# A one-token attention and SwiGLU layer on one core: the first 2 MiB of wq in eight DMAs of 16 partitions, and the last batch of K in one DMA

## The chip, the core and the metric

The kernel runs on one core of one Trainium2 chip. The core has five instruction streams: TensorE (PE, with its weight loads shown apart as PEld), VectorE (DVE), ScalarE (ACT), GpSimd (POOL) and SyncE (SP). SP does no arithmetic here; it issues DMAs. The transfers themselves are carried out by 16 DMA engines, which move data between the chip's memory (HBM) and the on-chip SBUF of 128 partitions. The metric is the device time of one execution in microseconds; lower is better. The kernel before takes 140.36 us (median of three runs, 140.25 to 140.44).

## The reference

Four sequences, one new token each (B = 4, D = 1024). Layer norm, attention over the last 2048 positions of a cache with 32 query heads and 4 key/value heads of 128 values, output projection and residual; then layer norm, a SwiGLU block of width 3584, and residual. Everything is bfloat16.

```python
def _A_ref(x, k_cache, v_cache, wq, wo):
    W = min(4096, max(256, Sk // 4))                      # 2048 of Sk = 8192
    q = (x @ wq).reshape(B, Sq, Hq, Dh).transpose(0, 2, 1, 3)
    k = jnp.repeat(k_cache[:, :, Sk - W:, :], rep, axis=1)
    v = jnp.repeat(v_cache[:, :, Sk - W:, :], rep, axis=1)
    scores = jnp.einsum("bhqd,bhkd->bhqk", q, k) * (Dh ** -0.5)
    o = jnp.einsum("bhqk,bhkd->bhqd", softmax(scores), v)
    return o.transpose(0, 2, 1, 3).reshape(B, Sq, Hq * Dh) @ wo

def _B_ref(x, w1, w3, w2):
    return (silu(x @ w1) * (x @ w3)) @ w2

h  = x + _A_ref(layernorm(x), k_cache, v_cache, wq, wo)
h2 = h + _B_ref(layernorm(h), w1, w3, w2)
```

With four rows of activations, nearly all the bytes are weights and cache: 8 MiB of wq, 8 of K, 8 of V, 8 of wo, 7 each of w1, w3 and w2, some 55.6 MB in all, each byte used once.

## The kernel before, in words

All large transfers are issued by SP, from one list called `plan` (line 131), in the order wq, K, V, wo, w1, w3, w2. Each entry fills one of five SBUF slots of 4 MiB (the pool `stream`, line 58; `SLOT` is 16384 bfloat16 per partition). `load_next` (line 143) takes the next entry; the first five are issued at once (line 152) and the others each time TensorE has been through the tile that an earlier slot held, so SP waits there for TensorE.

`load_rows` (line 92) loads weights, one DMA for each number in `pieces`. Its view of a weight, `(p i) n -> p (i n)`, gives each partition a contiguous run of rows. The first entry of wq is two DMAs of 2 MiB (`pieces` is `[2, 2]`): 128 partitions with 16 KiB each. The second is one of 4 MiB. `load_k` (line 103) loads two batches of K into a slot, one DMA of 2 MiB each; in partition `pp * 4 + g` lie 64 consecutive positions of head `g`, 16 KiB. For the last batch this is cut: the first 60 positions go as before (line 112), and the last `JT = 4` positions, 1 KiB per partition, go in a second DMA (line 114) whose access pattern names the head first, `g pp x` instead of `pp g x`. This one puts position block `pp` of head `g` into partition `g * 32 + pp`, so for these four columns the partitions are in another order, and line 259 reads them with another pattern.

ACT issues five small DMAs at the start: the input x (line 151) and four pieces of x in another layout (line 162).

Every DMA counts its completion on a semaphore. There are eight for all the DMAs of SP and ACT, given out in turn in the order of the program; a DMA whose semaphore was used by an earlier one is issued only after that earlier one has landed. In the kernel before, the order is x, the first DMA of wq, the four pieces of x, the second and third DMA of wq, and then K: the first DMA of K waits for x, the second for the first DMA of wq, and so on.

TensorE's work follows the same order: the query projection (line 224), K transposed in blocks of eight (line 278) and copied out by DVE and ACT in turn (lines 282 and 284), the scores one unit behind (`emit_scores`, line 252, 16 units of 512 positions), softmax, the product with V (line 330), wo (line 357), w1 and w3 (line 406), w2 (line 436). In `emit_scores`, a unit is four matmuls of 512 columns, one per head; the last unit is four of 384 and four of 128, because of the other partition order in its last four columns.

Of the kernel before, what the change touches and what calls it, by code (L numbers as in the profile page):

```python
# [10 lines left out]
P = 128  # L11
# [8 lines left out]
def kernel(  # L20
# [13 lines left out]
    nc = tc.nc  # L34

    B, _, D = A_x.shape
    Hkv, Sk, Dh = A_k_cache.shape[1], A_k_cache.shape[2], A_k_cache.shape[3]
    Hq = A_wq.shape[1] // Dh
    REP = Hq // Hkv
    W = min(4096, max(256, Sk // 4))  # L40
# [26 lines left out]
    QD = P // JG  # L67
# [6 lines left out]
    IF = F // P  # L74
    PK = P // Hkv
    JK = W // PK
    JT = 4
    assert CQ == REP * Dh and HF <= 512 and CG == QD * KC and CF == QD * IF and IO == QD == Hq


# [11 lines left out]
    def load_rows(src, n, r0, pieces):  # L92

        t = stream.tile([P, SLOT], BF16, tag="s")
        i = 0
        for m in pieces:
            nc.sync.dma_start(  # L97
                out=t[:, i * n : (i + m) * n], in_=src[:, (r0 + i) * n : (r0 + i + m) * n]
            )
            i += m  # L100
        return [t[:, k * n : (k + 1) * n] for k in range(i)]

    def load_k(b):
        t = stream.tile([P, SLOT], BF16, tag="s")
        out = []
        for k in range(BS):


            v = t[:, k * JK * Dh : (k + 1) * JK * Dh]
            n = (JK - JT) * Dh if b + k == B - 1 else JK * Dh  # L110
            k_v = A_k_cache[b + k, :, Sk - W : Sk, :].rearrange("g (pp j) d -> pp g (j d)", pp=PK)
            nc.sync.dma_start(out=v[:, :n], in_=k_v[:, :, :n])
            if n < JK * Dh:
                nc.sync.dma_start(out=v[:, n:], in_=k_v.rearrange("pp g x -> g pp x")[:, :, n:])
            out.append(v)
        return out

    def load_v(b):
# [11 lines left out]
    N_Q, N_F = Hq * Dh, F  # L130
    plan = (
        [("wq", load_rows, (wq_v, N_Q, c, [2, 2] if c == 0 else [4])) for c in range(0, KC, RQ)]
        + [("k", load_k, (b,)) for b in range(0, B, BS)]
        + [("v", load_v, (b,)) for b in range(0, B, BS)]
        + [("wo", load_rows, (wo_v, D, c, [RO])) for c in range(0, IO, RO)]
        + [("w1", load_rows, (w1_v, N_F, c, [RQ])) for c in range(0, KC, RQ)]
        + [("w3", load_rows, (w3_v, N_F, c, [RQ])) for c in range(0, KC, RQ)]
        + [("w2", load_rows, (w2_v, D, 0, [16])), ("w2", load_rows, (w2_v, D, 16, [5, 4, 2, 1]))]
    )
    loaded = {}  # L140
    cursor = [0]
# [19 lines left out]
    for j in range(JG):  # L161
        nc.scalar.dma_start(
            out=x_q[QD * j : QD * (j + 1) : RS, :], in_=x_flat[:, j * CG : (j + 1) * CG]
# [7 lines left out]
    for c in range(2):  # L171
# [8 lines left out]
        out=xn[:], in0=x_sb[:], scalar1=mv[:, 0:1], scalar2=rstd[:, 0:1],  # L180
# [4 lines left out]
    for kc in range(KC):  # L185
# [8 lines left out]
    qz = act.tile([P, B, Hkv * QD + REP], BF16)  # L194
# [6 lines left out]
        out=perm[:].rearrange("p (h dq) -> p h dq", dq=JG),  # L201
        in_=ident[:].rearrange("p (dq h) -> p h dq", dq=JG),
# [7 lines left out]
    for j in range(2, JG):  # L210
        nc.vector.tensor_tensor(
            out=same[:, 0, :], in0=same[:, 0, :], in1=ident[:, j * QD : (j + 1) * QD], op=ALU.add
# [6 lines left out]
    for kc in range(KC):  # L219
        wq_t = loaded["wq"][kc]  # L220
        for hf in range(CQ // 512):
            for g in range(JG):
# [3 lines left out]
                    lhsT=xnT[:, kc, :],  # L226
                    rhs=wq_t[:, c0 : c0 + 512],
                    start=(kc == 0),
                    stop=(kc == KC - 1),
# [7 lines left out]
    for r in range(REP):  # L237
        nc.tensor.transpose(out=qt_ps[:, r, :], in_=q_sb[:, r * Dh : (r + 1) * Dh], identity=ident[:])  # L238
    nc.vector.tensor_copy(
        out=qz[:, :, : Hkv * QD].rearrange("p b (g z) -> p b g z", g=Hkv)[:, :, :, :REP],  # L240
        in_=qt_ps[:].rearrange("p r (g x) -> p x g r", g=Hkv)[:, :B, :, :],
# [4 lines left out]
    scores_ps = psA.tile([P, W], FP32, tag="scores")  # L246
    NJ = 512 // PK
    TB = 8
    units = [(b, n) for b in range(B) for n in range(NSB)]
    kT_tiles = []  # L250

    def emit_scores(u):
        b, n = units[u]
        js = NJ - JT if u == len(units) - 1 else NJ
        for j0, j1 in ((0, js), (js, NJ)):
            if j0 == j1:
                continue
            kT_v = kT_tiles[u][:, j0:j1, :].rearrange(
                "d j (pp g) -> d g j pp" if j0 == 0 else "d j (g pp) -> d g j pp", g=Hkv
            )  # L260
            for g in range(Hkv):
                nc.tensor.matmul(  # L262
                    scores_ps[QD * g : QD * (g + 1), n * 512 + j0 * PK : n * 512 + j1 * PK],
                    lhsT=qz[:, b, g * QD : (g + 1) * QD],
                    rhs=kT_v[:, g, :, :],
                    start=(b == 0),
                    stop=(b == B - 1),
                    skip_group_check=True,
                )

    nt = 0
    for u, (b, n) in enumerate(units):
        k_v = loaded["k"][b].rearrange("p (j d) -> p j d", d=Dh)
        kT = ktpool.tile([P, NJ, P], BF16, tag="kT")
        for t in range(NJ // TB):
            kt_ps = psA.tile([P, TB, P], BF16, tag=f"kt{nt % 4}")
            for jj in range(TB):
                nc.tensor.transpose(  # L278
                    out=kt_ps[:, jj, :], in_=k_v[:, n * NJ + t * TB + jj, :], identity=ident[:]
                )  # L280
            if nt % 2 == 0:
                nc.vector.tensor_copy(out=kT[:, t * TB : (t + 1) * TB, :], in_=kt_ps[:])  # L282
            else:
                nc.scalar.copy(out=kT[:, t * TB : (t + 1) * TB, :], in_=kt_ps[:])  # L284
            nt += 1
        kT_tiles.append(kT)
        if u >= 1:
            emit_scores(u - 1)
        if n == NSB - 1 and b % BS == BS - 1:
            load_next()  # L290
    emit_scores(len(units) - 1)


# [9 lines left out]
        out=Pm[:].rearrange("q (c jq) -> q jq c", jq=NSB), in_=scores_ps[:].rearrange("q (jq c) -> q jq c", jq=NSB),  # L303
# [22 lines left out]
    for b in range(B):  # L326
        v_t = loaded["v"][b]
        for g in range(Hkv):
            for j in range(NK):
                nc.tensor.matmul(  # L330
                    OT_ps[:, b, g * REP : (g + 1) * REP],
                    lhsT=v_t[:, g, j, :],
                    rhs=PT_sb[:, j, g * QD + b * REP : g * QD + (b + 1) * REP],
                    start=(j == 0),
                    stop=(j == NK - 1),
# [19 lines left out]
    for i in range(IO):  # L355
        for j in range(JG):
            nc.tensor.matmul(  # L357
                y_ps[QD * j : QD * (j + 1), :],
                lhsT=o4[:, i, :, :].rearrange("p b s -> p (b s)"),
                rhs=loaded["wo"][i][:, j * CG : (j + 1) * CG],  # L360
                start=(i == 0),
                stop=(i == IO - 1),
# [26 lines left out]
        out=hn[:], in0=h1[:], scalar1=tot[:, 0:1], scalar2=rstd2[:, 0:1],  # L389
# [5 lines left out]
        out=hnT[:].rearrange("p k x -> p (k x)"), in_=hn[:].rearrange("q (c k) -> q k c", k=KC)  # L395
# [5 lines left out]
    def gate_up(kind, out_ps):  # L401
# [27 lines left out]
        out=hgT[:].rearrange("p i x -> p (i x)"),  # L429
        in_=hg[:].rearrange("q s c -> q (s c)").rearrange("q (c i) -> q i c", i=IF),  # L430
# [3 lines left out]
    for i in range(IF):  # L434
        for j in range(JG):
            nc.tensor.matmul(  # L436
                y2_ps[QD * j : QD * (j + 1), :],
                lhsT=hgT[:, i, :],
                rhs=loaded["w2"][i][:, j * CG : (j + 1) * CG],
                start=False,  # L440
                stop=(i == IF - 1),
                skip_group_check=True,
# [35 lines left out]
```

## Time and profile before

| what | value |
|---|---|
| median of three runs | 140.36 us |
| the profiled execution's own time | 140.44 us |
| its span, first to last instruction | 138.4 us |
| around the span | 2.0 us |
| TensorE matmul busy | 69.9 us, 50% of the span |
| VectorE, ScalarE busy | 36.4 us, 29.2 us |
| bytes read from HBM | 55.59 MB, 402 GB/s over the span |
| share of the 16 DMA engines' span that SP's queue used | 95.3% |
| granted TensorE clock, mean | 0.775 |

The span runs from the first to the last instruction of the program; the profiled execution's own time is about 2 us more. Of the engines none is busy for much more than half of the span, while the queue of SP's DMAs occupies the DMA engines for nearly all of it. A DMA is cut into packets, each carried by one of the 16 engines; the trace records the start, length and size of every packet, and each engine's part of a DMA ends in a 4-byte packet that counts on the semaphore. "Landed" below means that this count arrived.

### The profile page before, as it was taken

What the parts mean: (1) busy time and instruction counts of PE and PEld (TensorE: products, weight loads), DVE (VectorE), ACT (ScalarE), POOL (GpSimd) and SP (SyncE); (2) the same over time, 40 slices, a digit from 0 to 9 for tenths busy, and PEclk for the clock granted to TensorE, in tenths of its full rate; (3) what the DMA queues carried; (4) which work ended last, traced back from release to release, by engine and by line L of the source; (5) the groups of instructions that cost most, each with busy time, mean ns of one, the idle gap of its engine ahead of it and who ended that gap; (6) DMA issues with size and microseconds to landing.
All of it is one profiled execution on the core that took longest, in us unless ns stands there. A gap on an engine that the chain in (4) does not pass through costs nothing.

```text
span 138.4 us, 2316 instructions
## 1 busy us (share of the span) xinstructions
PE 69.9 (50%) x1049; PEld 44.7 (32%) x1049; DVE 36.4 (26%) x63; ACT 29.2 (21%) x28; POOL 1.6 (1%) x7
## 2 busy tenths in 40 slices
PE   0152204799898989500595687136080440801940
PEld 0111001296565646200585565112030210301820
DVE  6430000133343434440400203500003980070001
ACT  0400000125473736449450000000006000000000
POOL 4000000000000000000000000000000000000000
PEclk9999999999999999955555559955559555595685
DMA  5999989999999999999999999999999999899940
GB/s 154 441 414 511 426 388 398 445 426 421 432 402 339 419 419 421 417 462 497 398 426 403 436 439 421 456 423 414 439 456 411 414 439 477 379 432 408 418 186 2
DMA packets 4905, 55.74 MB, mean 403 GB/s; under 512 B 380, under 2 KB 540, under 8 KB 2848
## 3 DMA queue, kind: packets, MB, share of 16 engines
q1 hardware_dynamic: 4856, 55.58, 95.3%
q8 instruction: 8, 0.13, 0.3%
q10 hardware_dynamic: 40, 0.02, 0.1%
q14 instruction: 1, 0.01, 0.0%
HBM read 55.59 MB, written 0.01 MB: 402 GB/s over the span
## 4 chain that ended last, share of the span: by engine, by line
DMA 68%; PE 23%; ACT 4%; SPq 1%; DVE 1%; issue 1%; ACTq 0%
DMA t<-in_B_w_dram 53%; DMA t<-in_A_wq_dram 15%; PE kt_ps L278 11%; PE scores_ps L262 5%; ACT kT L284 4%; PE q_ps L224 3%; PE g_ps L406 2%; SPq L97 1%; PE qt_ps L238 1%; PE y_ps L436 1%; DVE q_sb L234 1%; DVE res L446 0%; ACTq L284 0%
## 5 line engine op out<-in xcount | busy, mean ns | idle before, releaser
L284 ACT COPY kT<-kt_ps 128x1024 bf16<-128x1024 bf16 x16 | 16.0, 1013 | 13.8 <-PE kt_ps L278 13.8
L278 PE MATMUL kt_ps<-ident,t 128*128 128x128 bf16 x256 | 18.3, 232 | 0.0
L278 PEld LDWEIGHTS <-t 128*128 128x128 bf16 x256 | 16.0, 105 | 6.1 <-issue 6.1
L282 DVE COPY kT<-kt_ps 128x1024 bf16<-128x1024 bf16 x16 | 11.1, 692 | 16.9 <-PE kt_ps L278 16.9
L406 PEld LDWEIGHTS <-hnT 128*32 128x32 bf16 x128 | 5.4, 139 | 27.6 <-issue 25.3
L224 PE MATMUL q_ps<-t,xnT 128*4 128x512 bf16 x64 | 7.3, 623 | 11.9 <-DMA t<-in_A_wq_dram 11.9
L262 PE MATMUL scores_ps<-kT,qz 128*32 128x512 bf16 (+2 forms) x68 | 10.5, 581 | 2.8 <-ACT kT L284 2.8
L406 PE MATMUL u_ps<-t,hnT 128*32 128x448 bf16 x64 | 6.2, 569 | 10.8 <-DMA t<-in_B_w_dram 10.8
L406 PE MATMUL g_ps<-t,hnT 128*32 128x448 bf16 x64 | 6.2, 563 | 10.5 <-DMA t<-in_B_w_dram 10.5
L436 PE MATMUL y_ps<-t,hgT 128*32 128x256 bf16 x112 | 5.7, 368 | 8.6 <-DMA t<-in_B_w_dram 8.6
L330 PE MATMUL OT_ps<-PT_sb,t 128*128 128x8 bf16 x256 | 7.4, 168 | 1.8 <-issue 1.6
L330 PEld LDWEIGHTS <-t 128*128 128x128 bf16 x256 | 7.3, 104 | 2.0 <-issue 1.8
L436 PEld LDWEIGHTS <-hgT 128*32 128x32 bf16 x112 | 4.3, 127 | 10.4 <-issue 6.3
L224 PEld LDWEIGHTS <-xnT 128*4 128x4 bf16 x64 | 2.0, 111 | 16.3 <-issue 16.0
L316 PE MATMUL pt_ps<-Dm,Pm 128*128 128x128 bf16 x16 | 1.9, 311 | 9.3 <-DVE Dm L309 9.3
L420 DVE RECIPROCAL eg<-eg 128x896 f32<-128x896 f32 x1 | 5.8, 5752 | 0.0
L357 PE MATMUL y_ps<-t,o 128*32 128x256 bf16 x128 | 5.1, 337 | 0.8 <-DVE o L346 0.8
L234 DVE TENSOR_SCALAR q_sb<-q_ps 128x512 bf16<-128x512 f32 x1 | 0.7, 691 | 17.9 <-PE q_ps L224 17.9
L235 ACT ACTIVATE q_sb<-q_ps 128x512 bf16<-128x512 f32 x1 | 0.6, 597 | 21.4 <-DVE q_sb L234 21.4
L419 DVE TENSOR_SCALAR eg<-eg 128x896 f32<-128x896 f32 x1 | 0.6, 627 | 16.8 <-ACT eg L418 16.8
L302 ACT ACTIVATE Pm<-scores_ps,nmax 128x2048 bf16<-128x2048 f32 x1 | 4.8, 4784 | 0.0
L316 PEld LDWEIGHTS <-Pm 128*128 128x128 bf16 x16 | 1.6, 145 | 9.7 <-ACT Pm L302 9.7
(67 smaller groups left out, 39.8 us busy)
## 6 DMA issues: line engine op xcount, KB each, us to landing
t<-in_B_w_dram SPq DMA_DIRECT2D x4, 3584.0 KB, 34.3
t<-in_A_v_cache_dram SPq DMA_DIRECT2D x4, 2048.0 KB, 30.2
t<-in_A_wo_dram SPq DMA_DIRECT2D x2, 4096.0 KB, 27.5
t<-in_A_k_cache_dram SPq DMA_DIRECT2D x3, 2048.0 KB, 25.7
t<-in_A_wq_dram SPq DMA_DIRECT2D x2, 2048.0 KB, 9.5
t<-in_A_wq_dram SPq DMA_DIRECT2D x1, 4096.0 KB, 20.9
t<-in_B_w_dram SPq DMA_DIRECT2D x1, 4096.0 KB, 42.2
t<-in_A_k_cache_dram SPq DMA_DIRECT2D x1, 1920.0 KB
```

The costliest lines, as they stand in the source:

```text
L224: nc.tensor.matmul(q_ps[QD * g : QD * g + B, hf * 512 : (hf + 1) * 512], lhsT=xnT[:, kc, :], rhs=wq_t[:, c0 : c0 + 512], start=(kc == 0), ...
L262: nc.tensor.matmul(scores_ps[QD * g : QD * (g + 1), n * 512 + j0 * PK : n * 512 + j1 * PK], lhsT=qz[:, b, g * QD : (g + 1) * QD], rhs=kT_v ...
L278: nc.tensor.transpose(out=kt_ps[:, jj, :], in_=k_v[:, n * NJ + t * TB + jj, :], identity=ident[:])
L282: nc.vector.tensor_copy(out=kT[:, t * TB : (t + 1) * TB, :], in_=kt_ps[:])
L284: nc.scalar.copy(out=kT[:, t * TB : (t + 1) * TB, :], in_=kt_ps[:])
L302: nc.scalar.activation(out=Pm[:].rearrange("q (c jq) -> q jq c", jq=NSB), in_=scores_ps[:].rearrange("q (jq c) -> q jq c", jq=NSB), func=A ...
L316: nc.tensor.matmul(pt_ps[:, jj, :], lhsT=Pm[:, (jb * JPB + jj) * P : (jb * JPB + jj + 1) * P], rhs=Dm[:], start=True, stop=True)
L330: nc.tensor.matmul(OT_ps[:, b, g * REP : (g + 1) * REP], lhsT=v_t[:, g, j, :], rhs=PT_sb[:, j, g * QD + b * REP : g * QD + (b + 1) * REP], ...
L357: nc.tensor.matmul(y_ps[QD * j : QD * (j + 1), :], lhsT=o4[:, i, :, :].rearrange("p b s -> p (b s)"), rhs=loaded["wo"][i][:, j * CG : (j + ...
L406: nc.tensor.matmul(out_ps[QD * j : QD * (j + 1), hf, :HF], lhsT=hnT[:, k, :], rhs=loaded[kind][k][:, c0 : c0 + HF], start=(k == 0), stop=( ...
L420: nc.vector.reciprocal(out=eg[:], in_=eg[:])
L436: nc.tensor.matmul(y2_ps[QD * j : QD * (j + 1), :], lhsT=hgT[:, i, :], rhs=loaded["w2"][i][:, j * CG : (j + 1) * CG], start=False, stop=(i ...
```

## The change

Two parts. The first DMA of the program's list, 2 MiB of wq for 128 partitions, becomes eight DMAs, each for 16 partitions that lie eight apart (partitions 0, 8, 16, ..., 120; then 1, 9, ...; to 7, 15, ..., 127), 16 KiB in each partition. All other calls of `load_rows` are as they were. And K's last batch is loaded by one DMA like the other three: the split of its last four columns is gone, from the load and from `emit_scores`, whose last unit is again four matmuls of 512 columns.

```diff
-    JT = 4
...
         for m in pieces:
-            nc.sync.dma_start(
-                out=t[:, i * n : (i + m) * n], in_=src[:, (r0 + i) * n : (r0 + i + m) * n]
-            )
+            step = 8 if cursor[0] == 0 and i == 0 else 1
+            for p0 in range(step):
+                nc.sync.dma_start(
+                    out=t[p0:P:step, i * n : (i + m) * n],
+                    in_=src[p0:P:step, (r0 + i) * n : (r0 + i + m) * n],
+                )
             i += m
...
-            n = (JK - JT) * Dh if b + k == B - 1 else JK * Dh
-            k_v = A_k_cache[b + k, :, Sk - W : Sk, :].rearrange("g (pp j) d -> pp g (j d)", pp=PK)
-            nc.sync.dma_start(out=v[:, :n], in_=k_v[:, :, :n])
-            if n < JK * Dh:
-                nc.sync.dma_start(out=v[:, n:], in_=k_v.rearrange("pp g x -> g pp x")[:, :, n:])
+            nc.sync.dma_start(
+                out=v,
+                in_=A_k_cache[b + k, :, Sk - W : Sk, :].rearrange("g (pp j) d -> pp g (j d)", pp=PK),
+            )
...
-        js = NJ - JT if u == len(units) - 1 else NJ
-        for j0, j1 in ((0, js), (js, NJ)):
-            if j0 == j1:
-                continue
-            kT_v = kT_tiles[u][:, j0:j1, :].rearrange(
-                "d j (pp g) -> d g j pp" if j0 == 0 else "d j (g pp) -> d g j pp", g=Hkv
-            )
-            for g in range(Hkv):
-                nc.tensor.matmul(
-                    scores_ps[QD * g : QD * (g + 1), n * 512 + j0 * PK : n * 512 + j1 * PK],
-                    lhsT=qz[:, b, g * QD : (g + 1) * QD],
-                    rhs=kT_v[:, g, :, :],
-                    start=(b == 0),
-                    stop=(b == B - 1),
-                    skip_group_check=True,
-                )
+        kT_v = kT_tiles[u][:].rearrange("d j (pp g) -> d g j pp", g=Hkv)
+        for g in range(Hkv):
+            z0 = (b * Hkv + g) * QD
+            nc.tensor.matmul(
+                scores_ps[QD * g : QD * (g + 1), n * 512 : (n + 1) * 512],
+                lhsT=qz[:, b, g * QD : (g + 1) * QD],
+                rhs=kT_v[:, g, :, :],
+                start=(b == 0),
+                stop=(b == B - 1),
+            )
```

SP issues 30 DMAs afterwards instead of 24: eight in place of one at the start, and one fewer in K. Since the eight semaphores are given out in turn, the waits at the start move too. Of the eight pieces the first three wait for nothing; the fourth waits for x, the fifth for piece 1, the sixth, seventh and eighth for the first, second and third small piece of x, and the second DMA of wq for the fourth small piece. The third DMA of wq then waits for piece 2, and the four DMAs of K for pieces 3 to 6. TensorE has eight fewer instructions (four weight loads and four matmuls).

## The prediction

> **What bounds the kernel now.** I read the slices first, then the chain of waits, then windows around the two edits, then SP's waits and the end of the timeline.
>
> ```profile
> PE   0152204799898989500595687136080440801940
> DMA  5999989999999999999999999999999999899940
> GB/s 154 441 414 511 426 388 398 445 426 421 432 402 339 419 419 421 417 462 497 398 426 403 436 439 421 456 423 414 439 456 411 414 439 477 379 432 408 418 186 2
> ```
>
> The DMA engines are busy from the first slice (3.46 us each) to the last but one; PE has holes everywhere. The chain of waits still hands a middle part to PE:
>
> ```profile
> 1.64 20.91 DMA t<-in_A_wq_dram
> ...
> 56.25 36.04 DMA t<-in_B_w_dram
> ...
> 96.40 37.66 DMA t<-in_B_w_dram
> ```
>
> Between 22.55 and 56.25 the chain runs through TensorE, because w1's first DMA is issued at 56.25, when TensorE gives a slot free. But it lands only 36 us later, behind transfers issued before it (wo's two DMAs land at 73 and 83). So TensorE could be many microseconds later without starving the queue. The end is the start of the byte stream, plus its length, plus a fixed tail. The tail starts where the last 256 KB of w2 land, at 134.69:
>
> ```profile
> 134.10 1.04 PE L436 MATMUL y_ps<-t,hgT 128*32 128x256 bf16 x12 [0.65 <-DMA t<-in_B_w_dram]
> ...
> 135.19 0.42 DVE L446 CAST res<-y_ps 128x256 bf16<-128x256 f32 x1 [11.55 <-PE y_ps L436]
> 135.64 0.61 SPq L447 DMA_DIRECT2D out_dram<-res  x1
> ```
>
> From 134.69 to the end of the span (138.40) it is 3.71 us, which the change does not touch.
>
> **The stream's own prices.** In the packet records a 16 KiB packet takes 611 ns (26.8 GB/s for one of the 16 engines), a 15 KiB one 573 ns, a 1 KiB one 46 ns where nothing disturbs it, a semaphore packet 9 ns. A 2 MiB DMA is eight 16 KiB packets per engine, 4.9 us. The windows show the one place where the stream sags after its start:
>
> ```profile
> 36.00:38.00 2.00, 2.00 (x32) 1.55 (x32) 0.69 (x1) 0.37 (x1) 0.00 (x0) 1.00 1.00 428
> ...
> 42.00:43.60 1.60, 1.00 (x10) 0.30 (x7) 0.14 (x1) 0.89 (x1) 0.00 (x0) 1.00 1.05 265
> 43.60:45.00 1.40, 1.40 (x27) 1.40 (x27) 0.69 (x1) 0.35 (x1) 0.00 (x0) 1.00 1.04 410
> ```
>
> The last columns are the share of DMA time and GB/s: 265 instead of 428 with every engine busy. It is the K remainder of line 114. Its 128 packets of 1 KiB lie on only four engines (four semaphore packets instead of sixteen), from 41.36 to 42.96; 0.6 us after its start V's 4 KiB packets on the other twelve go from 159 to between 270 and 300 ns, the 1 KiB packets from 46 to between 62 and 88, and all recover 0.6 us after its end. The four engines' counts arrive 0.8 to 0.9 us after their semaphore packets; elsewhere about 0.34. So data had been taken in and waited to be written: it is the SBUF side that was full.
>
> **Part one, K: gained.** For twelve engines V's first DMA took 5.61 to 5.66 us against 4.97 for its second: 0.64 too long. They also get back their share of K's last rows, 8 x (611 - 573) = 0.30 us. Net -0.33. The four engines of the remainder need 6.87 us from the end of K's main part to the end of V's first DMA, which becomes 4.97 + 0.30: -1.6. Following packets by their ends (the next begins 3 to 4 ns before), the landings of w2's last piece are: four engines by 132.53, eleven from 133.68 to 133.93, one at 134.69. Eight of the eleven are ordinary engines that each carried one of the eight 16 KB instruction fetches (some 1.4 us each); three are remainder engines. The one at 134.69 is the fourth, which also met an 8 KB fetch at 83.59. With -1.6 it drops to 133.1, and the eight set the end at 133.93 - 0.33 = 133.6: -1.1 us. If V's slow start had another cause, they end at 133.93 + 0.30 = 134.2: -0.46. I take -1.1, since the sag has the remainder's length and place. TensorE's last unit (four matmuls near 0.6 us instead of four of 384 and four of 128 columns) is hidden behind a queue of over 25 us; without that cover it would be some tenths of a microsecond.
>
> **Part two, the eight pieces.** Bytes and packets are the same; seven more semaphore packets per engine are 7 x 9 ns = 0.06 us. Nothing starts earlier: the first DMA is issued at 0.73 and its first packet starts at 1.75, while x, with four packets, is issued at 0.74 and starts at 1.68. Two costs have no row of their own.
>
> The first is SP's waiting. Now:
>
> ```profile
> SPq L112 <- DMA t<-in_A_wq_dram: 5.0, 1, 5.0
> ...
> SPq L112 <- DMA x_sb<-in_A_x_dram: 0.2, 1, 0.2
> ```
>
> Here SP sat 5 us for a landing with 10 MiB issued, and the engines stayed busy. With pieces, piece 4 waits for x (landed 2.39), piece 5 for piece 1 (by 3.6), pieces 6 to 8 and wq's second DMA for x's four small pieces, which landed at 7.3, 8.1, 9.2 and 10.4 because on their four engines they stood behind 16 KiB packets. Behind the waiting SP stands all of wq, K and V. But with short queues the small pieces pass sooner: five pieces keep the engines until 1.75 + 1.2 (the first packet) + 4 x 0.61 = 5.4, by then nothing stands before the small ones, and they land by 5.75 (0.34 later); piece 6 then starts about 1 us after its issue, at 6.8. So the stall is 0 to 1.4 us; I take 0.1, as each engine's small packets should slip in between two pieces, and none if the pieces are slow.
>
> The second is the rate. A piece names 16 partitions, eight apart, so the 16 engines write to a part of SBUF at a time. The normal row is 611 ns per packet: 0. The row of the only large DMA here that confines engines to few partitions is the K remainder: 32 KiB per engine from 41.37 to 43.90, less the usual 0.34, is 2.2 us, or 14.9 GB/s instead of 26.8. At that rate eight packets take 8 x 1.10 = 8.8 us instead of 4.9: +3.9. The window's 265 GB/s would make 7.9 us, +3.0; without taking off the 0.34, 10.1 us, +5.2. I take +3.9: strided pieces on a write-limited side are nearer to the remainder than to a DMA of all partitions, though 1 KiB packets are not 16 KiB ones.
>
> [...]
>
> Sum: +3.9 + 0.06 - 1.1 = +2.9 us. The profiled execution took 140.44, span 138.40 and 2.04 around, 0.08 above the median; on the median 140.36 this is 143.3.
>
> **Rivals.**
>
> *Full rate, 0.27.* If the sag came from 1 KiB packets or from HBM, 16 KiB pieces run at 611 ns each, and the K gain remains: -1.1 + 0.16 = -0.9, 139.4 (139.0 to 140.2 with the -0.46 and a short stall). For it: 16 KiB is the size that runs at 26.8 GB/s everywhere else. Against it: the counts of the remainder came late, which a slow read would not do. This is the faster side, and it decides wherever the pieces cost less than 1.0 us.
>
> *SP starves the engines, 0.10.* The pieces run at full rate but are issued too late: stall 1.4, or up to 3 if half the engines have nothing until piece 5 arrives (its issue 3.6 plus 1.0, against 1.75). With -1.1 to -0.46 that is 140.6 to 142.5, middle 141.5. For it: the waits for x's small pieces, 7.3 to 10.4 before. Against it: these were late because of the queue that is now absent.
>
> *The split does nothing visible* is part of the first rival: its gain is then K's alone.
>
> **How the numbers follow.** Slow pieces 0.63, time 143.3, its own range 142.3 (+3.0 - 1.1) to 145.0 (+5.2 - 0.46). Full rate 0.27, starved 0.10. About 0.2%, 0.28 us, is what a measurement here tells from no change: of the full-rate case 0.23 is faster and 0.04 within; of the starved case 0.01 is within. Faster 0.23, same 0.05, slower 0.72. The range has to take in the middle of the full-rate case: 139.3 to 145.0, leaving out less than 2 in 10.
>
> **What would show it.** Slow pieces: the first two slices of GB/s near 150 and 240, q_ps waiting for wq's first rows until about 11.5 to 12 instead of 8.14, the second landing about 4 later than 12.92, all later landings shifted alike. Full rate: first matmul of L224 near 8. Starved: DMA digits under 9 in the second slice. K: no window near 42 to 46 below 400 GB/s, and the end less late than the start by about 1 us. I am wrong if the pieces go at 428 GB/s, or if the sag near V's first DMA stays without the remainder.

## The result, and the profile after

The changed kernel takes 145.0 us (median of six runs, 144.16 to 145.88) against 140.33: 1.033 of the kernel before, 95% interval 1.028 to 1.039. The prediction said slower, by 2.9 us to 143.3; it is slower by 4.67 us, just past the top of the stated range, which is 4.64 us (145.0 on 140.36). The six times are not spread evenly: three lie at 144.2 to 144.3 and three at 145.7 to 145.9. Runs more than 1.5% above the fastest of the same kernel are left out of the ratios, here one of 148.91 us, of the pieces alone. The profiled execution belongs to the lower group: 144.16 us, span 142.2.

The 40 slices of the changed kernel, busy share of the DMA engines in tenths and GB/s (a slice is 3.55 us):

```profile
DMA  5998999999999999999999999999999999998950
GB/s 141 224 221 300 447 443 433 396 420 443 438 438 391 416 421 422 416 423 527 443 406 410 424 408 459 408 444 436 411 444 432 420 436 486 415 424 365 424 229 2
```

The engines are as busy as before, yet the second and third slice move 224 and 221 GB/s where the kernel before had 441 and 414. An engine counts as busy for as long as its packet takes, and here a 16 KiB packet takes 1.22 us instead of 0.61. In finer windows of the changed kernel (the last two columns are DMA share and GB/s; a window counts a packet's bytes and time where the packet begins, so a short one scatters):

```profile
3.50:5.50 2.00, 0.00 (x0) 0.00 (x0) 0.31 (x2) 1.38 (x2) 0.00 (x0) 1.00 1.07 223
5.50:7.50 2.00, 0.64 (x8) 0.56 (x8) 1.28 (x7) 0.19 (x1) 0.00 (x0) 1.00 0.88 199
7.50:9.50 2.00, 0.00 (x0) 0.00 (x0) 0.91 (x6) 0.00 (x0) 0.00 (x0) 1.00 1.05 229
9.50:12.00 2.50, 0.00 (x0) 0.00 (x0) 0.00 (x0) 0.00 (x0) 0.00 (x0) 1.00 0.96 216
12.00:14.00 2.00, 0.79 (x8) 0.27 (x12) 0.00 (x0) 0.00 (x0) 0.00 (x0) 1.00 0.88 360
```

Half the rate until the eight pieces are through, near 12 us. The packet records say it packet by packet: from 3.4 to 10.9 us a 16 KiB packet takes 1222 ns at the median, where it took 611 before. TensorE's first matmuls on wq (timeline of the changed kernel) show what is late:

```profile
13.21 1.88 PE L225 MATMUL q_ps<-t,xnT 128*4 128x512 bf16 x16 [6.07 <-DMA t<-in_A_wq_dram]
18.06 1.88 PE L225 MATMUL q_ps<-t,xnT 128*4 128x512 bf16 x16 [2.97 <-DMA t<-in_A_wq_dram]
27.75 3.58 PE L225 MATMUL q_ps<-t,xnT 128*4 128x512 bf16 x32 [7.81 <-DMA t<-in_A_wq_dram]
```

Before, these stood at 8.14, 12.92 and 22.59: 5.1 us later, each of them. The end of the timeline has the same form as before, with the last piece of w2 at 138.35 instead of 134.69, 3.7 us later:

```profile
137.78 1.02 PE L431 MATMUL y_ps<-t,hgT 128*32 128x256 bf16 x12 [0.78 <-DMA t<-in_B_w_dram]
138.84 0.42 DVE L441 CAST res<-y_ps 128x256 bf16<-128x256 f32 x1 [11.62 <-PE y_ps L431]
139.29 0.70 SPq L442 DMA_DIRECT2D out_dram<-res  x1
```

So of 5.1 us lost in the first 18 us, about 1.5 came back by the end. And SP's own waits in the changed kernel name a new kind:

```profile
SPq L99 <- DMA x_q<-in_A_x_dram: 2.3, 2, 1.7
SPq L99 <- DMA t<-in_A_wq_dram: 1.3, 1, 1.3
```

SP waits for the small pieces of x between the pieces of wq, as the order of the semaphores said it would.

### The profile page after: what moved, and what is told of

Same layout as the page of the kernel before. It is cut to its first block, busy times and chain, and to the rows that moved or that the text cites. A ratio compares the mean times of both kernels' runs of the same rounds, so it can differ in the third digit from the quotient of the medians.

```text
span 142.2 us, 2317 instructions
## 1 busy us (share of the span) xinstructions
PE 68.9 (48%) x1045; PEld 43.6 (31%) x1045; DVE 36.3 (26%) x63; ACT 29.0 (20%) x28; POOL 1.6 (1%) x7
## 4 chain that ended last, share of the span: by engine, by line
DMA 69%; PE 19%; ACT 5%; ACTq 2%; SPq 1%; issue 1%; DVE 1%
DMA t<-in_B_w_dram 52%; DMA t<-in_A_wq_dram 13%; PE kt_ps L273 8%; ACT kT L279 5%; PE scores_ps L258 5%; DMA x_q<-in_A_x_dram 4%; PE q_ps L225 3%; PE g_ps L401 2%; SPq L99 1%; ACTq L163 1%; PE y_ps L431 1%; DVE q_sb L235 0%; ACT q_sb L236 0%; ACTq L152 0%; DVE res L441 0%
## 5 line engine op out<-in xcount | busy, mean ns | idle before, releaser
L273 PE MATMUL kt_ps<-ident,t 128*128 128x128 bf16 x256 | 16.5, 219 | 0.0
L273 PEld LDWEIGHTS <-t 128*128 128x128 bf16 x256 | 14.4, 98 | 5.0 <-issue 4.9
L258 PE MATMUL scores_ps<-kT,qz 128*32 128x512 bf16 x64 | 9.9, 609 | 3.1 <-ACT kT L279 3.1
L325 PEld LDWEIGHTS <-t 128*128 128x128 bf16 x256 | 7.3, 104 | 3.1 <-issue 3.0
L352 PE MATMUL y_ps<-t,o 128*32 128x256 bf16 x128 | 6.4, 394 | 0.8 <-DVE o L341 0.8
L352 PEld LDWEIGHTS <-o 128*32 128x32 bf16 x128 | 4.7, 141 | 2.5 <-DVE o L341 1.0
```

What stands on the lines that cost most here:

```text
L258: nc.tensor.matmul(scores_ps[QD * g : QD * (g + 1), n * 512 : (n + 1) * 512], lhsT=qz[:, b, g * QD : (g + 1) * QD], rhs=kT_v[:, g, :, :], ...
L273: nc.tensor.transpose(out=kt_ps[:, jj, :], in_=k_v[:, n * NJ + t * TB + jj, :], identity=ident[:])
L325: nc.tensor.matmul(OT_ps[:, b, g * REP : (g + 1) * REP], lhsT=v_t[:, g, j, :], rhs=PT_sb[:, j, g * QD + b * REP : g * QD + (b + 1) * REP], ...
L352: nc.tensor.matmul(y_ps[QD * j : QD * (j + 1), :], lhsT=o4[:, i, :, :].rearrange("p b s -> p (b s)"), rhs=loaded["wo"][i][:, j * CG : (j + ...
```

## The experiments

Three theories stood against each other. The write side: a DMA that names few partitions is written more slowly than one that names all 128, as the prediction read it from the K remainder (265 GB/s in its window). The number: eight DMAs cost by their issue and SP's waits. The K part: whether its remainder was worth 1.1 us. All ratios are to the kernel before, run on the same chip beside them.

**K alone.** The changed kernel with one DMA for wq's first 2 MiB.

```diff
-            step = 8 if cursor[0] == 0 and i == 0 else 1
+            step = 1
```

> The changed kernel with wq's first 2 MiB in one DMA of 128 partitions again; K's last batch stays in one DMA. My sum for the K part alone: the sag at 42 to 43.6 us goes (no window there under 400 GB/s), twelve engines gain 0.33 us and the four of the remainder 1.6 us, so 140.3 - 1.1 = 139.2. If the sag is V's own start: 139.9. If K's part brings nothing: 140.3.

139.4 us (139.27 to 139.46), ratio 0.993 [0.992, 0.994]: 1.0 us faster than the kernel before. The windows where that one had 265 GB/s:

```profile
41.30:42.00 0.70, 0.70 (x12) 0.34 (x9) 0.64 (x1) 0.20 (x1) 0.00 (x0) 1.00 0.92 375
42.00:43.60 1.60, 1.00 (x12) 0.38 (x9) 0.05 (x1) 0.81 (x1) 0.00 (x0) 1.00 1.02 415
43.60:45.00 1.40, 1.40 (x29) 1.40 (x27) 0.69 (x1) 0.44 (x1) 0.00 (x0) 1.00 1.01 407
```

The sag of 265 is gone (375 is a window of 0.7 us, in which few packets begin; with each packet's bytes spread over its duration it is 422). The last piece of w2 lands at 133.51 instead of 134.69. So K's part gave what it was priced at, and the pieces alone must cost some 5 to 6 us.

**The pieces alone.** The kernel before with wq's first DMA cut in eight and K's remainder kept.

```diff
+            step = 8 if cursor[0] == 0 and i == 0 else 1
+            for p0 in range(step):
+                nc.sync.dma_start(
+                    out=t[p0:P:step, i * n : (i + m) * n],
+                    in_=src[p0:P:step, (r0 + i) * n : (r0 + i + m) * n],
+                )
```

> The kernel before with wq's first 2 MiB in eight DMAs of 16 partitions; K's remainder stays. If the two parts add up and K is worth 1.1 us, 145.4 (5.1 us later than before, as wq's second DMA lands 5.1 us later in the changed kernel); if K is worth nothing, 144.2 to 145. The sag should be seen again, 5 us later.

Four runs: 144.66, 145.21, 146.02 and 148.91 us. Without the last the ratio is 1.035 [1.030, 1.040], about 145.4 us. It fits a sum of two parts, but its times are as scattered as those of the changed kernel, so 1.0 us between the two can't be read from it. The sag came back, some 5 us later and flatter (windows of the 148.91 us execution):

```profile
47.00:48.60 1.60, 1.00 (x8) 0.19 (x4) 0.26 (x1) 1.01 (x1) 0.00 (x0) 1.00 1.02 320
48.60:50.00 1.40, 1.40 (x29) 1.39 (x26) 0.67 (x1) 0.23 (x1) 0.00 (x0) 1.00 0.97 345
```

**Eight DMAs by columns.** As many DMAs, of the same size, with the same waits; each has all partitions.

```diff
+            parts = 8 if cursor[0] == 0 and i == 0 else 1
+            cw = m * n // parts
+            for c in range(parts):
+                nc.sync.dma_start(
+                    out=t[:, i * n + c * cw : i * n + (c + 1) * cw],
+                    in_=src[:, (r0 + i) * n + c * cw : (r0 + i) * n + (c + 1) * cw],
+                )
```

> The changed kernel, its eight DMAs cut by columns instead of partitions: each has all 128 partitions and 2 KiB in each. Same number of DMAs, same waits of SP. [...] Number of DMAs and SP's waits: 144 to 146 as in the changed kernel, first matmul near 13.

142.31 us (141.95 to 142.58), ratio 1.014 [1.011, 1.017]: under the 144 to 146 that was expected from the number of DMAs, and over the 139.9 of full rate, an estimate from 139.4 for K alone and 64 packets of 84 ns (2 KiB, in the kernel before) in place of eight of 611. A miss for both theories. The first matmul comes early, at 7.21, but wq's second DMA is late (second matmul group at 15.70 instead of 12.88 in the kernel with K alone). Its windows:

```profile
3.50:5.50 2.00, 0.00 (x0) 0.00 (x0) 0.98 (x3) 1.58 (x2) 0.00 (x0) 1.00 0.81 253
5.50:7.50 2.00, 0.93 (x12) 0.67 (x16) 1.47 (x7) 0.00 (x0) 0.00 (x0) 1.00 0.88 274
7.50:9.50 2.00, 1.33 (x10) 0.29 (x3) 0.73 (x5) 0.00 (x0) 0.00 (x0) 1.00 1.05 343
```

Here the share is 0.81 and 0.88: the engines do run dry, by the packet records about 0.8 us each between 3 and 9 us. So SP's waits can cost something, when the pieces are quick (1.25 us, by the same kernel without them, below).

**Eight pieces of consecutive partitions.** Partitions 0 to 15, then 16 to 31, and so on.

```diff
+            parts = 8 if cursor[0] == 0 and i == 0 else 1
+            pw = P // parts
...
-                    out=t[p0:P:step, i * n : (i + m) * n],
-                    in_=src[p0:P:step, (r0 + i) * n : (r0 + i + m) * n],
+                    out=t[c * pw : (c + 1) * pw, i * n : (i + m) * n],
+                    in_=src[c * pw : (c + 1) * pw, (r0 + i) * n : (r0 + i + m) * n],
```

> The changed kernel, its eight DMAs with 16 consecutive partitions each (0 to 15, then 16 to 31, ...) instead of 16 that lie eight apart. Same number, size and waits. [...] Number of DMAs and SP's waits: as the changed kernel, 144 to 146. A cost of the stride of eight partitions itself: faster than the changed kernel.

151.11 us (two runs), ratio 1.077 [1.074, 1.079]. Same number, size and waits as in the changed kernel, 6 us slower. One window over the pieces of this kernel:

```profile
3.50:17.00 13.50, 0.66 (x8) 0.58 (x8) 3.33 (x15) 1.58 (x2) 0.00 (x0) 1.00 1.03 126
```

126 GB/s, packets of 2.10 us, where the changed kernel has 215 GB/s and 1.22 us. The rate goes with the partitions that a DMA names, and the number of DMAs, eight in both, can't explain it.

**The pieces without SP's waits.** The four small pieces of x are issued only after the query projection; the eight semaphores then fall so that pieces 1 to 7 wait for nothing.

```diff
-    nc.vector.memset(x_q[:], 0.0)
...
     nc.scalar.mul(out=q_sb[:, 512:], in_=q_ps[:, 512:], mul=qscale)
+    nc.vector.tensor_single_scalar(out=x_q[:], in_=q_sb[:, :CG], scalar=0.0, op=ALU.mult)
+    for j in range(JG):
+        nc.scalar.dma_start(
+            out=x_q[QD * j : QD * (j + 1) : RS, :], in_=x_flat[:, j * CG : (j + 1) * CG]
+        )
```

> The changed kernel with the four small pieces of x issued only after the query projection. The eight semaphores then fall so that pieces 1 to 7 wait for nothing, piece 8 for x and wq's second DMA for piece 1: no wait of SP for the small pieces. The changed kernel's own times fall in two groups, 144.2 to 144.3 and 145.7 to 145.9. If the upper group is SP waiting for a small piece that lands one 1.2 us packet later, there is one group here, at or under 144.2, with no idle DMA time after 3 us. If the groups come from elsewhere (instruction fetches meeting on one DMA engine), both remain. If SP's waits were all of the cost: near 139.5.

144.28 us (144.13 to 144.32, four runs), ratio 1.029 [1.027, 1.030]: one group only, at the place of the lower one. The window of its pieces, in step with the changed kernel's 215 for the same stretch:

```profile
3.50:11.00 7.50, 0.65 (x8) 0.57 (x8) 2.50 (x14) 0.29 (x1) 0.00 (x0) 1.00 1.01 210
```

The packet records show no idle engine between 3 and 18 us. Without a wait that costs anything the pieces still cost 144.28 - 139.4 = 4.9 us: that is the rate, with the later first packet (see the end). The later x was not tried beside one undivided DMA. That the upper group is missing points to the waits; the profiles of the changed kernel further down show how.

**Columns without SP's waits.** The same move of x in the kernel with eight DMAs by columns.

> Eight DMAs by columns (all 128 partitions, 2 KiB each) with the small pieces of x issued after the query projection. By columns alone was 142.3, 2.9 us over the kernel with one DMA (139.4), and its DMA engines were idle for about 1 us between 3 and 9 us. If that was SP waiting for landings, it is now 139.4 + 0.5 (64 packets of 84 ns) = 139.9. If eight DMAs cost this by themselves: 142.3 again.

141.06 us (140.6 to 141.52), ratio 1.007 [1.005, 1.009]. Between the two theories again: the waits explain 1.25 of the 2.9 us and not all. In both kernels by columns the 2 KiB packets of wq take 100 ns on the mean (84 at the median, some far longer), 6.4 us in all per engine instead of the 4.9 of 16 KiB packets. That is 1.5 of the 1.65 us left. Why single packets are so long is open.

**Two halves.** One DMA more than with K alone, 64 partitions each.

```diff
+            parts = 2 if cursor[0] == 0 and i == 0 else 1
+            pw = P // parts
...
+                    out=t[c * pw : (c + 1) * pw, ...], in_=src[c * pw : (c + 1) * pw, ...]
```

> The kernel with K whole, wq's first 2 MiB in two DMAs of 64 partitions (0 to 63, 64 to 127). Only one DMA more, almost no more waits. [...] Number of DMAs and waits: 139.4 to 139.7.

144.40 us (two runs), ratio 1.030 [1.028, 1.032]: as slow as eight pieces without waits (144.28). Window of this kernel:

```profile
3.50:11.00 7.50, 0.66 (x8) 0.57 (x8) 2.52 (x14) 1.58 (x2) 0.00 (x0) 1.00 1.01 210
```

Two DMAs cost what eight do. The number of DMAs is out as the cause of the halved rate.

**Every second partition.** Again two DMAs of 64 partitions, now the even ones and the odd ones.

```diff
-            step = 8 if cursor[0] == 0 and i == 0 else 1
+            step = 2 if cursor[0] == 0 and i == 0 else 1
```

> K whole, wq's first 2 MiB in two DMAs of 64 partitions that lie two apart (even ones, then odd ones). [...]

139.64 us (139.58 to 139.86), ratio 0.995 [0.993, 0.997]: near K alone (139.4), far from the two halves (144.40). Its window over the two DMAs:

```profile
3.50:6.50 3.00, 0.07 (x1) 0.07 (x2) 1.12 (x6) 1.58 (x2) 0.00 (x0) 1.00 1.03 438
```

Full rate, 611 ns per packet. This is the sharpest pair of the study: 64 partitions, two DMAs, packets of 16 KiB in both, 210 GB/s for 0 to 63 and 438 for every second one. The remaining 0.25 us over K alone goes with the first packet, which starts at 2.10 instead of 1.74.

One rival is not separated by any of these edits. The rows of partition p lie p times 64 KiB into wq, so a choice of partitions is also a choice of HBM addresses, and the reads could be the slow side. On the author's reading the counts speak against it. The 16 four-byte packets of the first DMA end at 2.88 to 3.66 us in the changed kernel, and their counts arrive at 3.67 to 4.53, some 0.8 to 0.9 us later. For 0 to 63 it is 6.80 to 7.91 and 7.73 to 8.71, for 16 consecutive partitions 2.63 to 3.91 and 4.47 to 5.25; for every second partition 5.07 to 5.65 and 5.40 to 5.98, only 0.33 us. So the counts come 0.8 to 1.8 us after their packets where the pieces are slow, and 0.33 us where they are not. The author takes late counts for data that waited to be written, which would make the write the slow side. No run shows how late a count comes after a slow read, and a run that changes the addresses alone was not made.

**K's remainder on all engines.** wq in one DMA; K's last four columns in their own DMA with the same 1 KiB packets, in the order of the main part.

```diff
-                nc.sync.dma_start(out=v[:, n:], in_=k_v.rearrange("pp g x -> g pp x")[:, :, n:])
+                nc.sync.dma_start(out=v[:, n:], in_=k_v[:, :, n:])
```

> wq in one DMA; K's last four columns again in a DMA of their own, with the same 1 KiB packets, but in the order of the main part (position block first), so that it runs on all 16 engines. If the sag of the kernel before came from four engines that write to few partitions: no window under 400 GB/s there, 139.4 to 139.6. If 1 KiB packets made it: the sag is back and the time near 140.0 to 140.4.

139.46 us (139.39 to 139.5), ratio 0.994 [0.993, 0.996], and no sag:

```profile
40.00:41.30 1.30, 1.30 (x24) 1.00 (x20) 0.44 (x2) 0.80 (x1) 0.00 (x0) 1.00 0.82 333
41.30:42.00 0.70, 0.50 (x4) 0.09 (x1) 0.29 (x1) 0.66 (x1) 0.00 (x0) 1.00 1.14 455
42.00:43.60 1.60, 1.20 (x16) 0.75 (x16) 0.00 (x0) 0.35 (x1) 0.00 (x0) 1.00 1.02 415
```

The remainder runs from 40.9 us on. The 333 of the first window is under the 400 of the expectation, but it only counts few packets beginning: spread over their durations it is 417, and each of the 128 packets of 1 KiB took 46 or 47 ns. It was not the 1 KiB packets that cost 1 us in the kernel before but the order that put them on four engines. The fewer engines and the other partitions at a time came together, and these runs don't separate them.

**The changed kernel again, twice.** To see an execution of the upper group.

> The changed kernel itself, once more, to see one of its slower executions in a profile. If its two groups of times (144.2 and 145.8) come from SP waiting, a profile of the upper group has the sixth piece issued about 1.2 us later than 5.62 (when the first small piece of x lands one slow packet later), DMA engines idle between 7 and 11 us, and wq's second DMA landing about 1.5 us later than 18.0; one of the lower group is as before.

> The same again, for the same reason: either group, with the sixth piece issued near 5.6 us in the lower and near 6.9 us in the upper one.

The first profile is of 146.23 us, the second of 144.55. SP's issues of pieces in the timeline of the slower one (the fifth and the sixth piece):

```profile
4.61 0.49 SPq L99 DMA_DIRECT2D t<-in_A_wq_dram  x1
...
7.00 0.49 SPq L99 DMA_DIRECT2D t<-in_A_wq_dram  x1
```

The sixth piece goes out at 7.00; in the two quicker profiles at 5.62 and 6.03, as in the one of 144.16 us (sixth and seventh piece in one row):

```profile
5.62 2.73 SPq L99 DMA_DIRECT2D t<-in_A_wq_dram  x2
```

It waits for the first small piece of x, which landed at 6.99 here and at 5.60 and 6.02 there. Its data packets start at about the same time in all three (4.02 to 4.53 here, 3.92 to 4.70 there), but its four-byte packets, which count, start at 5.33 to 5.84 here and at 3.96 to 4.74 there: one slow packet of wq more stood before them. The share of DMA time then falls after 10 us (window of the slower one):

```profile
10.00:13.00 3.00, 0.00 (x0) 0.00 (x0) 0.00 (x0) 0.00 (x0) 0.00 (x0) 1.00 0.79 180
```

Adding up the gaps in the packet records, an engine sits idle 0.65 us on the mean between 7 and 15 us, against about 0.1 in the two quicker profiles. The second matmul group stands at 19.78 instead of 18.06, 1.7 us later, and the execution is 2.1 us longer than 144.16. The mean hides a few late engines: 14 of the 16 counts of wq's second DMA are in by 18.8, the last two at 19.70 and 19.73 (17.66 for 15 and 18.02 for the last in the execution of 144.16). Why these two fall behind is open.

**Another order of the pieces.** Pieces in the order 0, 4, 1, 5, 2, 6, 3, 7, so that the first partitions of neighbours in the queue lie three or four apart instead of one. No run before this one bears on the order of the pieces.

```diff
-            for p0 in range(step):
+            for p0 in ((0, 4, 1, 5, 2, 6, 3, 7) if step == 8 else (0,)):
```

> [...]

145.57 us (two runs), ratio 1.037 [1.034, 1.040]: no gain in time, but the rate did move. From 3.4 to 6.5 us a 16 KiB packet takes 1.09 us at the median, from then to 10.9 us 1.00, against 1.23 and 1.20 in the changed kernel, and the first matmul on wq starts at 13.00 instead of 13.21. The gain is lost behind waits like those of the upper group: the sixth piece goes out at 6.38, an engine sits idle 1.0 us on the mean between 7 and 15 us, and the second matmul group stands at 19.37. What this order gives without the waits was not tried.

## Why the prediction was right in kind and short in size

*What bounds the kernel.* Right. The 5.1 us lost by 18 us are in every later landing of wq, and TensorE being later by as much showed nowhere else.

*K's part, -1.1.* Right: -1.0 alone, the sag gone, gone too with the same small packets on all engines, and back when the remainder is. That the sag was the remainder, and not V's own start, is shown; that its cause is the write side is the author's reading of the late semaphore counts (0.8 to 0.9 us, elsewhere about 0.34), and no run shows it.

*Nothing starts earlier.* Right, and a little worse: the first packet of wq starts at 2.14 instead of 1.75, a loss of 0.25 to 0.4 us for which the sum had no term.

*The rate, +3.9.* The pieces are slow, as predicted, but the cost was sized too small. This is the first step that failed: the prediction took 14.9 GB/s per engine from the K remainder, 8 x 1.10 us. Measured are 1.22 us per packet, half the normal rate, and 4.9 us for the pieces without waits (late start included). So the first matmul on wq came at 13.21, where the prediction expected 11.5 to 12. Taking off the usual 0.34 us of landing delay had made the row look quicker than the state it shows (without it the prediction had +5.2); the row was also a mixture: 84 of the 128 packets of 1 KiB still took 46 or 47 ns, before the sag set in, and the other 44 took 48 to 88. No row of the first trace could tell 0 to 63 from every second partition, which ran at 210 and 438 GB/s.

*SP's waits, +0.1.* The second step that failed. The prediction took it that slow pieces hide the waits. They do in the lower group: none of the 4.9 us goes when the waits go. But whether the count of the first small piece of x passes before or behind one more slow packet differs from execution to execution, and the executions of the upper group are 1.4 to 2 us longer. Five of the ten executions of the changed kernel are in it, and the median of the first six, 145.0, lies between the groups, 0.8 above the lower one. The stall that the prediction put at 0 to 1.4 us and then took as 0.1, and as none for slow pieces, was in truth a part of the likeliest case. That the late piece makes this difference rests on three profiles of the changed kernel and on the one group without the waits.

*The sum.* For the lower group, -1.0 for K, +4.9 for rate and late start: 140.3 + 3.9 = 144.2, as measured. For the upper group 1.5 more. The middle of the two groups is +4.7: against the predicted +2.9 the rate took about 1.0 more, the waits 0.8, and K gave 0.1 less.

*Its arithmetic.* The 0.1 for SP's waits was named but stands in no sum of the slow case (+3.9 + 0.06 - 1.1). The top of the range, called +5.2 - 0.46, is 145.1 on 140.36 and not 145.0, and held no stall at all. Two bounds of the rivals don't follow from their terms either: no term gives the 139.0, and 3 - 0.46 makes 142.9, not 142.5. The result turns on neither of these last two.

The version that beats both kernels is the one with K whole and wq in one DMA: 139.4 us.

## What to carry to other kernels

In a kernel that streams at full DMA rate, price a split DMA first by the partitions that each part names. Here 16 neighbours ran at 126 GB/s, 64 neighbours at 210, 16 partitions eight apart at 215, and every second partition at 438, with the 611 ns per 16 KiB packet that a DMA of all 128 partitions has. The size of the packets comes next: the parts by columns, with all 128 partitions but 2 KiB packets, still cost 1.65 us without waits. And where DMAs take completion semaphores in turn, look up which small, late DMA a large one will wait for: a split moves every wait behind it.

## What the runs showed that was not expected

- Busy DMA engines at half rate: share 1.00 with 215 GB/s over 7.5 us. The share alone does not show it; the GB/s beside it do.
- The first DMA's first packet starts at 1.74 to 1.76 us with 128 or 16 consecutive partitions, and at 2.10 to 2.16 with 16 or 64 strided ones or with 0 to 63. SP's issuing instruction took 0.38 to 0.39 us in the first kind and 0.58 to 0.64 in the second, so a part of it is a longer issue; why was not tried.
- One small DMA of 2 KB, whose tile is first read at 90.9 us, goes with about 1.5 us of the whole time through the semaphore it shares.
